# First-layer blocks in pairs: one SiLU and one block transposition over two PSUM banks

## Chip, cores and metric

The kernel runs on one core of one Trainium2 chip. Its metric is the device time of one execution in microseconds (us); the time stated for a kernel is the median of several runs. The engines are called as the profile calls them: PE (matmuls), PEld (the loading of a matmul's stationary operand, which overlaps PE), DVE (VectorE), ACT (ScalarE), POOL (GpSimd) and SP (the queue that issues the DMAs).

## The reference

A long convolution by FFT over 8 sequences of 3072 tokens with 256 channels, then a dense layer pair on all 24576 tokens, then a soft mixture of experts. Cut to what matters:

```python
X = np.fft.rfft(x, axis=1);  y = np.fft.irfft(X * (filt_r + 1j * filt_i)[None], n=3072, axis=1)
x = y.reshape(24576, 256)
h = x @ w_in                                  # 256 -> 2048
g = h * (1.0 / (1.0 + np.exp(-h)))            # SiLU
x = g @ w_out                                 # 2048 -> 256
logits = x @ phi                              # 256 -> 32 slots
d = softmax of logits over the tokens;  slot_input = d.T @ x
slot_out = per expert: relu(slot_input @ w1[e]) @ w2[e]        # 8 experts, 4 slots each
c = softmax of logits over the slots;  out = c @ slot_out
```

## The kernel before

The second dense layer is never formed for all tokens: its weights are folded with `phi` into `wp`, so that logits come straight from the SiLU outputs, and the sum over tokens is taken over the 2048 hidden values.

**Tiling.** Tokens go in 48 chunks of 512, six to a sequence. A chunk's first layer has 16 blocks m = 0 to 15 of 128 hidden values. `hidden(c, m)` makes one block: six matmuls of 128x512 into one PSUM bank of the tag "ph" (four banks). `act(c, m)` is one SiLU on ACT from that bank to a tile `g` in SBUF (tag "g", 12 buffers). `turn(c, m)` transposes `g` in blocks of 32x32 on DVE into the tile `X`. `logits(c, h)` multiplies eight `g` tiles with `wp`; `soft0` and `soft1` make the running maximum and the exponentials of the chunk (`nm`, `e`, `E`), and `dsum`, `update` the weighted sum of `X` (`pd`, `acc`). `hidden` of block m can begin only when the SiLU of block m-4 has read the bank.

**Staging.** The FFT of the next sequence runs between these blocks: `mat1` (tiles `pa`, evicted by `out1` to `ea`), `mat2` (`px`, scaled by `scale` on ACT, DVE and POOL), `mat3` (`pb`, four banks, evicted on ACT by four instructions to `eb` in `out3`). `pa`, `px` and three of the `pb` banks share three PSUM banks of the tag "pf". By the plan `mat3` stands in chunks 2 to 5, 8 to 11, and so on to 38 to 41: in 28 chunks, each time behind block 3. The exponentials of a chunk (`soft1`) are taken in the next chunk, also near block 3, and need another ACT function table than SiLU: each time a table load before and one behind. In every fourth chunk (4, 8, ... 44) a further Exp over 512 columns (`cexp`, tile `ct`) comes in there.

**What sets the order.** `at(t, fn, ...)` collects all steps with a due time in units of one block; they are written out sorted by time, and PE executes exactly that order. On ACT, DVE, POOL and SP the order is chosen by the framework's scheduler when the program is built; each of these engines then works strictly in that order. Semaphores and buffer rotation are generated.

**Tail.** After the last chunk the experts run once: `peh` (tag "ph"), ReLU to `hr`, transposition through PE (`pht`), copy to `hT`, second product (`pso`), split into `so` by quarters q. The slot softmax, parked in DRAM as `cT`, is loaded back as `cl` (tag "g") and split into `z`. The output product `po` (576 matmuls of 256 columns) alternates between "ph" and "pf" banks; DVE evicts the one half and ACT the other.

Of the kernel before, what the change touches and what calls it, by code (L numbers as in the profile page):

```python
# [27 lines left out]
CPB = NJ // JC  # L28
NB16 = TC // 32

BUFS = dict(X=2, yT=2, g=12, L=2, nm=4, E4=2, lall=2, ct=1, cm=1,
            ld=3, c=2, ch=2, xh=2, ev=2, a=2, f=2, sw=1, y=4, ev8=1, bl=1, dl=1, wt=3)


# [6 lines left out]
def fftconv_moe_softmoe(ctx, tc, x, cmat, dmat, emat, gmat, filt, filt0, w_in, w_outT,  # L41
# [6 lines left out]
    cst = ctx.enter_context(tc.tile_pool(name="cst", bufs=1))  # L48
    wk = ctx.enter_context(tc.tile_pool(name="wk", bufs=2))
    dram = ctx.enter_context(tc.tile_pool(name="dram", bufs=2, space=bass.MemoryType.DRAM))  # L50
    ps_h = ctx.enter_context(tc.tile_pool(name="ps_h", bufs=4, space=bass.MemoryType.PSUM))
    ps_1 = ctx.enter_context(tc.tile_pool(name="ps_1", bufs=1, space=bass.MemoryType.PSUM))
    ps_f = ctx.enter_context(tc.tile_pool(name="ps_f", bufs=3, space=bass.MemoryType.PSUM))
    fctx = ctx.enter_context(ExitStack())
# [94 lines left out]
    def at(t, fn, *args):  # L149
        plan.append((t, len(plan), fn, args))  # L150
# [148 lines left out]
    def fft_first():  # L299
# [4 lines left out]
        def load(v):  # L304
            tag = ("y", "y", "y", "y", "sw", "f")[v]
            cs[v] = fp.tile([P, 4, P], F32, tag=tag, bufs=BUFS[tag], name=f"c_0_{v}")
            DQ.dma_start(cs[v], cmat[:, 4 * v:4 * v + 4, :])
            for i in range(2):
                xs[2 * v + i] = wk.tile([P, 2, CH], F32, tag="g", bufs=BUFS["g"], name=f"x_0_{2 * v + i}")
                DQ.dma_start(xs[2 * v + i], xb[:, 4 * v + 2 * i:4 * v + 2 * i + 2, :])  # L310

        def loadf(i):
# [32 lines left out]
                scale(ps[r], f[:, r], y, sw, Q + U == 0)  # L345

        def second(Q):
            ps = [ps_h.tile([P, 2, CH], F32, tag="ph", name=f"pb_0_{Q}{g}") for g in range(4)]
            stage3(ps, [ys.pop((Q, U)) for U in range(4)], Q)
            if Q % 3:  # L350
                ev = wk.tile([P, 2, 4, CH], F32, tag="yT", bufs=BUFS["yT"], name=f"eb_0_{Q}")
            else:
                ev = fp.tile([P, 2, 4, CH], F32, tag="ev8", bufs=BUFS["ev8"], name=f"eb_0_{Q}")
            for g, p in enumerate(ps):
                A.activation(ev[:, :, g, :], p, AF.Copy)  # L355
            store2(s2k, ev, Q)
# [71 lines left out]

    def hidden(c, m):
        y = ytile[c]  # L430
        ph = ps_h.tile([P, TC], F32, tag="ph", name=f"ph_{c}_{m}")
        n = 0
        for h in range(2):
            for a, k in ((0, 0), (0, 1), (1, 0)):
                mm(ph, w_hl[:, a, h, m * P:(m + 1) * P], y[:, h, k, :], n == 0, n == 5)
                n += 1
        pht[c, m] = ph

    def act(c, m):
# [124 lines left out]
    for c in range(NCHUNK):  # L564
        t0 = 16 * c
        ty = t0 - 4.4 if c else -2
        if c > 0:
            at(ty - 3.8, loadd, c)
            at(ty - 3.8, load3, c)
        for h in range(2):  # L570
            at(ty + 0.8 * h, mat4, c, h)
            at(ty + 0.8 * h + 0.55, out4, c, h)
        for m in range(NM):
            t = t0 + m
            at(t, hidden, c, m)
# [249 lines left out]
```

## Time and profile before

| | before |
|---|---|
| median of 3 runs (lowest, highest) | 2046.39 us (2046.02, 2047.71) |
| the profiled execution, its own time | 2049.17 us |
| its span, first to last instruction | 2047.4 us |
| PE busy | 1926.2 us, 94% of the span |
| DVE busy | 1149.6 us, 56% |
| ACT busy | 966.8 us, 47% |
| POOL busy | 337.9 us, 17% |
| mean granted share of the TensorE clock | 0.965 |

All durations below come from the one profiled execution. Its own time is 1.8 us over its span and 2.8 us over the median. A "busy" PE is one whose modelled matmuls overlap without a gap. In rows of the timeline the first number is the start in us, the second the length in us; several instructions that follow each other are one row with a count, and a bracket names the idle time of the engine before it and who ended it. The first 130 us are the first sequence's FFT, the chunks run from there to 1935, the rest is the tail.

### The profile page before, as it was taken

What the parts mean: (1) busy time and instruction counts of PE and PEld (TensorE: products, weight loads), DVE (VectorE), ACT (ScalarE), POOL (GpSimd) and SP (SyncE); (2) the same over time, 40 slices, a digit from 0 to 9 for tenths busy, and PEclk for the clock granted to TensorE, in tenths of its full rate; (3) what the DMA queues carried; (4) which work ended last, traced back from release to release, by engine and by line L of the source; (5) the groups of instructions that cost most, each with busy time, mean ns of one, the idle gap of its engine ahead of it and who ended that gap; (6) DMA issues with size and microseconds to landing.
All of it is one profiled execution on the core that took longest, in us unless ns stands there. A gap on an engine that the chain in (4) does not pass through costs nothing. (4 is left out here: it accounts for less than half of the span.)

```text
span 2047.4 us, 53590 instructions
## 1 busy us (share of the span) xinstructions
PE 1926.2 (94%) x23264; PEld 1468.1 (72%) x23264; DVE 1149.6 (56%) x1950; ACT 966.8 (47%) x1833; POOL 337.9 (17%) x249
## 2 busy tenths in 40 slices
PE   3448999999999999999999999999999999999798
PEld 2237777777777777877777777777777777778568
DVE  1475556556566565565565566566565564554444
ACT  1344445445455454554554545545555454444234
POOL 1465111211121111211221112112121110000000
PEclk7668999999999999999999999999999999999899
DMA  9655332534244333443354334424343335110659
GB/s 291 181 178 182 87 103 81 168 119 111 80 135 139 100 104 109 157 110 88 89 160 121 101 99 131 143 82 124 86 139 95 94 95 179 39 35 24 231 206 384
DMA packets 179308, 265.08 MB, mean 129 GB/s; under 512 B 16272, under 2 KB 115712, under 8 KB 174848
## 3 DMA queue, kind: packets, MB, share of 16 engines
q1 hardware_dynamic: 179072, 261.64, 42.0%
q8 instruction: 183, 3.00, 0.6%
q14 instruction: 53, 0.43, 0.1%
HBM read 177.69 MB, written 83.89 MB: 128 GB/s over the span
## 5 line engine op out<-in xcount | busy, mean ns | idle before, releaser
L60 PE MATMUL ph<-yT,w_hl 128*128 128x512 f32 x4608 | 1153.3, 399 | 2.8 <-ACT g L441 1.9
L60 PEld LDWEIGHTS ph<-yT,w_hl 128*128 128x128 f32 x4608 | 837.6, 188 | 256.3 <-issue 77.6
L451 DVE STREAM_TRANSPOSE X<-g 128x512 f32<-128x512 f32 x768 | 530.0, 702 | 421.6 <-ACT g L441 419.6
L441 ACT ACTIVATE g<-ph 128x512 f32<-128x512 f32 x768 | 449.1, 604 | 665.8 <-PE ph L60 645.2
L182 POOL TENSOR_TENSOR sw<-sw,f 128x512 f32<-128x512 f32 x128 | 166.7, 1304 | 985.6 <-ACT sw L176 925.0
L60 PE MATMUL pd<-X,E 32*32 32x512 f32 x6144 | 221.8, 604 | 7.2 <-DMA E<-ed 7.2
L515 DVE SCALAR_TENSOR_TENSOR acc<-acc,nm,pd 128x512 f32<-128x512 f32 x188 | 127.8, 741 | 121.6 <-PE pd L60 121.6
L60 PE MATMUL pl<-g,wp 128*32 128x128 f32 x6144 | 187.6, 274 | 1.9 <-DVE acc L515 1.6
L60 PEld LDWEIGHTS pl<-g,wp 128*32 128x32 f32 x6144 | 161.8, 110 | 35.7 <-issue 19.4
L221 POOL TENSOR_TENSOR xh<-x,xh 128x512 fp32r<-128x512 f32 x84 | 123.8, 1474 | 352.5 <-DVE xh L220 348.9
L60 PEld LDWEIGHTS pd<-X,E 32*32 32x32 f32 x6144 | 119.3, 103 | 83.0 <-issue 43.4
L60 PEld LDWEIGHTS py<-d,b 128*128 128x128 f32 x768 | 101.8, 194 | 30.4 <-DMA b<-s 22.9
L60 PE MATMUL py<-d,b 128*128 128x128 f32 x768 | 102.6, 277 | 22.0 <-DMA b<-s 22.0
L181 DVE TENSOR_TENSOR y<-px,f 128x512 f32<-128x512 f32 x120 | 82.5, 691 | 60.1 <-ACT sw L176 46.2
L175 ACT ACTIVATE sw<-px 128x256 f32<-128x256 f32 x128 | 49.4, 386 | 138.1 <-DVE y L183 105.1
L183 DVE TENSOR_TENSOR y<-y,sw 128x512 f32<-128x512 f32 x128 | 93.7, 736 | 35.8 <-POOL sw L182 32.3
L60 PE MATMUL px<-a,em 48*32 48x256 f32 x2048 | 76.8, 399 | 30.1 <-DMA a<-s 20.4
L60 PE MATMUL pb<-y,gm 32*64 32x256 f32 x2048 | 73.3, 412 | 22.5 <-ACT eb L355 11.9
L60 PEld LDWEIGHTS px<-a,em 48*32 48x32 f32 x2048 | 33.1, 109 | 66.2 <-issue 35.8
L60 PE MATMUL pa<-xh,ch 128*128 128x256 f32 x504 | 76.8, 287 | 3.7 <-ACT ch L223 2.3
L60 PEld LDWEIGHTS pb<-y,gm 32*64 32x64 f32 x2048 | 47.0, 141 | 45.5 <-DVE y L183 14.9
L60 PEld LDWEIGHTS pa<-xh,ch 128*128 128x128 f32 x504 | 71.2, 191 | 11.6 <-ACT ch L223 3.6
(113 smaller groups left out, 1190.2 us busy)
## 6 DMA issues: line engine op xcount, KB each, us to landing
f<-in_filt_dram SPq DMA_DIRECT2D x112, 256.0 KB, 2.9
x<-in_x_dram SPq DMA_DIRECT2D x96, 256.0 KB, 3.5
s<-ea SPq DMA_DIRECT2D x96, 256.0 KB, 3.5
s<-eb SPq DMA_DIRECT2D x64, 384.0 KB, 5.1
b<-s SPq DMA_DIRECT2D x48, 512.0 KB, 4.2
out_dram<-ots SPq DMA_DIRECT2D x24, 1024.0 KB, 5.8
a<-s SPq DMA_DIRECT2D x112, 192.0 KB, 3.9
wt<-in_w_dram SPq DMA_DIRECT2D x14, 1024.0 KB, 12.1
```

The source lines that it names most:

```text
L60: T.matmul(o, lhsT=l, rhs=r, start=start, stop=stop)
L175: A.activation(sw[:, 0, :], p[:, 1, :], AF.Copy, scale=-1.0)
L181: V.tensor_tensor(y, p, f[:, 0, :].unsqueeze(1).to_broadcast([P, 2, CH]), op=ALU.mult)
L182: G.tensor_tensor(sw, sw, f[:, 1, :].unsqueeze(1).to_broadcast([P, 2, CH]), op=ALU.mult)
L183: V.tensor_tensor(y, y, sw, op=ALU.add)
L221: G.tensor_tensor(h[:, 1, :], tf, h[:, 0, :], op=ALU.subtract)
L441: A.activation(g, pht.pop((c, m)), AF.Silu)
L451: V.transpose(xt[c][:, m].rearrange("p b j -> p (b j)"), gt[c, m])
L515: V.scalar_tensor_tensor(out=acc[:, :, a, :], in0=acc[:, :, a, :], scalar=mrun[c][:, 3:4], in1=p, op0=ALU.mult, op1=ALU.add)
```

## The change

Two blocks share one tile of two banks. `hidden` still writes one block per call into its own bank. `act` and `turn` are called for odd m only, with the pair's first block, and take 1024 columns at once; `logits` reads halves of the pair's `g`. The tag "ph" has 2 buffers of two banks in place of 4 of one, the tag "g" 6 buffers of 1024 columns in place of 12 of 512. Other users of these tags follow: the first sequence's `x` and `pb`, the experts' `peh` (one tile for both halves n), and `po` of the output (one tile for the two products on "ph"). The tiles `hr`, `hT`, `nT`, `cl` keep 512 columns, and each takes one of the six "g" buffers.

```diff
-BUFS = dict(X=2, yT=2, g=12, L=2, ...
+BUFS = dict(X=2, yT=2, g=6, L=2, ...
-    ps_h = ctx.enter_context(tc.tile_pool(name="ps_h", bufs=4, space=bass.MemoryType.PSUM))
+    ps_h = ctx.enter_context(tc.tile_pool(name="ps_h", bufs=2, space=bass.MemoryType.PSUM))
...
     def hidden(c, m):
         y = ytile[c]
-        ph = ps_h.tile([P, TC], F32, tag="ph", name=f"ph_{c}_{m}")
+        if m % 2 == 0:
+            pht[c] = ps_h.tile([P, 2, TC], F32, tag="ph", name=f"ph_{c}_{m}")
...
-                mm(ph, w_hl[:, a, h, m * P:(m + 1) * P], y[:, h, k, :], n == 0, n == 5)
+                mm(pht[c][:, m % 2, :], w_hl[:, a, h, m * P:(m + 1) * P], y[:, h, k, :], n == 0, n == 5)
...
     def act(c, m):
-        g = wk.tile([P, TC], F32, tag="g", bufs=BUFS["g"], name=f"g_{c}_{m}")
-        A.activation(g, pht.pop((c, m)), AF.Silu)
+        g = wk.tile([P, 2, TC], F32, tag="g", bufs=BUFS["g"], name=f"g_{c}_{m}")
+        A.activation(g, pht.pop(c), AF.Silu)
...
-        V.transpose(xt[c][:, m].rearrange("p b j -> p (b j)"), gt[c, m])
+        V.transpose(xt[c][:, m:m + 2].rearrange("p m b j -> p (m b j)"), gt[c, m].rearrange("p m t -> p (m t)"))
...
             at(t, hidden, c, m)
-            at(t + 0.5, act, c, m)
-            at(t + 1.2, turn, c, m)
+            if m % 2:
+                at(t + 0.5, act, c, m - 1)
+                at(t + 1.2, turn, c, m - 1)
...
     for r in range(2):
         hT = []
+        peh = ps_h.tile([P, 2, 512], F32, tag="ph", name=f"peh_{r}")
         for n in range(2):
-            ph = ps_h.tile([P, 512], F32, tag="ph", name=f"peh_{r}{n}")
+            ph = peh[:, n]
...
+        poh = ps_h.tile([P, 2, 2, CH], F32, tag="ph", name=f"po_{i}")
         for v in range(4):
             c = 2 * i + v // 2
-            po = (ps_h, ps_f)[v % 2].tile([P, 2, CH], F32, tag=("ph", "pf")[v % 2], name=f"po_{i}_{v}")
+            po = ps_f.tile([P, 2, CH], F32, tag="pf", name=f"po_{i}_{v}") if v % 2 else poh[:, v // 2]
```

PE's order in the chunks is the same. On ACT it moves. First ACT in chunk 16, a chunk with `mat3` and the further Exp: from the last SiLU ahead of the burst to the first behind it (`g_16_2` is the tile `g` of chunk 16, block 2; now of blocks 2 and 3). Before:

```order
L441 ACTIVATE g_16_2_8250<-ph_16_2_8230 128x512
L441 ACTIVATE g_16_3_8296<-ph_16_3_8252 128x512
L480 ACT_TABLE_LOAD
L480 ACTIVATE e_15_8237,nm_15_8225<-lall_3_6894,nm_15_8225 128x128
L482 ACTIVATE nm_15_8225<-nm_14_7770,nm_15_8225 128x1
L530 ACTIVATE ct_3_8348<-ct_3_8348 128x512
L272 ACTIVATE eb_3_2_8298<-pb_3_20_8260 128x2x256
L272 ACTIVATE eb_3_2_8298<-pb_3_21_8261 128x2x256
L272 ACTIVATE eb_3_2_8298<-pb_3_22_8262 128x2x256
L272 ACTIVATE eb_3_2_8298<-pb_3_23_8263 128x2x256
L441 ACT_TABLE_LOAD
L441 ACTIVATE g_16_4_8313<-ph_16_4_8305 128x512
```

And now, on the same engine at the same place:

```order
L444 ACTIVATE g_16_2_7762<-ph_16_2_7699 128x1024
L483 ACT_TABLE_LOAD
L483 ACTIVATE e_15_7706,nm_15_7694<-lall_3_6459,nm_15_7694 128x128
L485 ACTIVATE nm_15_7694<-nm_14_7271,nm_15_7694 128x1
L533 ACTIVATE ct_3_7806<-ct_3_7806 128x512
L272 ACTIVATE eb_3_2_7764<-pb_3_20_7726 128x2x256
L272 ACTIVATE eb_3_2_7764<-pb_3_21_7727 128x2x256
L272 ACTIVATE eb_3_2_7764<-pb_3_22_7728 128x2x256
L272 ACTIVATE eb_3_2_7764<-pb_3_23_7729 128x2x256
L444 ACT_TABLE_LOAD
L444 ACTIVATE g_16_4_7785<-ph_16_4_7771 128x1024
```

The burst between the two SiLU places is the same; one SiLU of 1024 columns stands on each side of it where two of 512 stood.

Second, ACT in chunk 12, where the further Exp meets `mat1` (`pa` to `ea`, `c` to `ch`). Before:

```order
L480 ACT_TABLE_LOAD
L480 ACTIVATE e_11_6455,nm_11_6439<-lall_2_5018,nm_11_6439 128x128
L482 ACTIVATE nm_11_6439<-nm_10_5942,nm_11_6439 128x1
L441 ACT_TABLE_LOAD
L441 ACTIVATE g_12_3_6494<-ph_12_3_6477 128x512
L530 ACT_TABLE_LOAD
L530 ACTIVATE ct_2_6572<-ct_2_6572 128x512
L239 ACTIVATE ea_3_6_6513<-pa_3_6_6496 128x512
L223 ACTIVATE ch_3_8_6519<-c_3_8_6446 128x256
L441 ACT_TABLE_LOAD
L441 ACTIVATE g_12_4_6511<-ph_12_4_6503 128x512
L441 ACTIVATE g_12_5_6537<-ph_12_5_6522 128x512
```

And now:

```order
L483 ACT_TABLE_LOAD
L483 ACTIVATE e_11_6052,nm_11_6036<-lall_2_4711,nm_11_6036 128x128
L485 ACTIVATE nm_11_6036<-nm_10_5571,nm_11_6036 128x1
L533 ACTIVATE ct_2_6158<-ct_2_6158 128x512
L444 ACT_TABLE_LOAD
L444 ACTIVATE g_12_2_6088<-ph_12_2_6045 128x1024
L239 ACTIVATE ea_3_6_6105<-pa_3_6_6090 128x512
L223 ACTIVATE ch_3_8_6111<-c_3_8_6043 128x256
L444 ACTIVATE g_12_4_6127<-ph_12_4_6097 128x1024
```

The further Exp now stands with the other one, between the same two table loads: two loads fewer here. SiLU of blocks 2 and 3, half of which stood before the burst, stands behind it.

Third, PE at the start of the output product in the tail (`po_i_v` before; now `po_i` is the "ph" tile of both v = 0 and v = 2). Before:

```order
L60 MATMUL po_0_0_22449<-so_22245,z_0_22397 128x256 x2
L60 MATMUL po_0_2_22465<-so_22245,z_0_22397 128x256 x2
L60 MATMUL po_1_0_22482<-so_22245,z_0_22397 128x256 x2
L60 MATMUL po_1_2_22498<-so_22245,z_0_22397 128x256 x2
L60 MATMUL po_0_0_22449<-so_22245,z_0_22397 128x256
```

And now:

```order
L60 MATMUL po_0_20897<-so_20695,z_0_20845 128x256 x2
L60 MATMUL po_1_20929<-so_20695,z_0_20845 128x256 x2
L60 MATMUL po_0_20897<-so_20695,z_0_20845 128x256
L60 MATMUL po_1_20929<-so_20695,z_0_20845 128x256
L60 MATMUL po_0_20897<-so_20695,z_0_20845 128x256 x2
```

Two products are begun side by side where four were: the second bank of a tile is written only after the first was evicted.

## Rows read from the trace of the kernel before

**Rows 1.** The page: span, and the first layer's matmuls (busy us, mean ns).

```profile
span 2047.4 us, 53590 instructions
...
L60 PE MATMUL ph<-yT,w_hl 128*128 128x512 f32 x4608 | 1153.3, 399 | 2.8 <-ACT g L441 1.9
```

**Rows 2.** Busy time by stage, 300 to 1700 us: the sum of four stages.

```profile
sum 1400.00, PE 1396.94 PEld 1058.13 DVE 829.04 ACT 710.66 POOL 236.18; mean PE 349.23 PEld 264.53 DVE 207.26 ACT 177.66 POOL 59.05
```

**Rows 3.** Waits of PE, 300 to 1900 us: us in total, times, longest.

```profile
PE pa L60 <- ACT ch L223: 2.3, 3, 0.8
PE ph L60 <- ACT g L441: 1.9, 2, 1.6
PE pl L60 <- DVE acc L515: 1.6, 2, 1.4
```

**Rows 4.** Groups by line, 300 to 1900 us: busy us, mean ns, idle before.

```profile
L451 DVE STREAM_TRANSPOSE X<-g 128x512 f32<-128x512 f32 x700 | 483.0, 702 | 381.0 <-ACT g L441 379.1
L441 ACT ACTIVATE g<-ph 128x512 f32<-128x512 f32 x701 | 409.8, 604 | 607.7 <-PE ph L60 589.0 <-DVE X L451 16.8
...
L485 DVE STREAM_TRANSPOSE e<-e 128x128 f32<-128x128 f32 x44 | 13.7, 311 | 52.1 <-ACT e L480 51.5
L467 ACT ACTIVATE lall<-pl 128x128 f32<-128x128 f32 x44 | 12.4, 282 | 23.7 <-PE pl L60 23.7
```

**Rows 5.** Timeline of chunk 16: table loads, SiLU behind the burst, and PE.

```profile
762.56 1.28 ACT L480 ACT_TABLE_LOAD   x1 [0.38 <-DVE nm L471]
...
763.39 7.21 PE L60 MATMUL ph<-yT,w_hl 128*128 128x512 f32 x30
...
767.02 1.28 ACT L441 ACT_TABLE_LOAD   x1
...
768.32 2.06 ACT L441 ACTIVATE g<-ph 128x512 f32<-128x512 f32 x4
```

**Rows 6.** Timeline of chunk 10, ACT and PE.

```profile
542.15 0.60 ACT L441 ACTIVATE g<-ph 128x512 f32<-128x512 f32 x1
...
539.62 7.30 PE L60 MATMUL ph<-yT,w_hl 128*128 128x512 f32 x30
```

**Rows 7.** Timeline of chunk 11, the last with a third FFT stage in its sequence.

```profile
574.95 1.28 ACT L480 ACT_TABLE_LOAD   x1 [0.60 <-DVE nm L471]
...
578.23 0.60 ACT L441 ACTIVATE g<-ph 128x512 f32<-128x512 f32 x1
578.73 2.06 ACT L272 ACTIVATE eb<-pb 128x512 f32<-128x512 f32 x4
...
579.78 0.87 PE L60 MATMUL pa<-xh,ch 128*128 128x256 f32 x6
```

**Rows 8.** Timeline of chunk 12, ACT and PE.

```profile
615.59 1.28 ACT L441 ACT_TABLE_LOAD   x1
...
618.80 0.63 ACT L530 ACTIVATE ct<-ct 128x512 f32<-128x512 f32 x1
...
617.95 1.55 PE L60 MATMUL ph<-yT,w_hl 128*128 128x512 f32 x6
620.27 1.20 PE L60 MATMUL pa<-xh,ch 128*128 128x256 f32 x6 [0.76 <-ACT ch L223]
```

**Rows 9.** Timeline of chunk 44, ACT and PE.

```profile
1799.80 2.07 ACT L441 ACTIVATE g<-ph 128x512 f32<-128x512 f32 x4
...
1800.45 1.66 PE L60 MATMUL ph<-yT,w_hl 128*128 128x512 f32 x6 [1.65 <-ACT g L441]
```

**Rows 10.** Timeline of the tail: PE on the experts, ACT on the quarters, SP.

```profile
1960.83 1.93 PE L60 MATMUL pso<-wt,hT 128*32 128x256 f32 x32 [0.69 <-ACT hT L678]
...
1970.82 0.37 ACT L689 ACTIVATE so<-pso 32x256 fp32r<-32x256 f32 x1 [1.55 <-PE pso L60]
...
1972.26 0.38 ACT L689 ACTIVATE so<-pso 32x256 fp32r<-32x256 f32 x1
...
1973.84 0.38 ACT L689 ACTIVATE so<-pso 32x256 fp32r<-32x256 f32 x1
...
1940.54 29.07 SPq L698 DMA_DIRECT2D cl<-cT  x12
```

More of the change, by code (lines that the diff above doesn't have):

```diff
@@ L29 @@
 NB16 = TC // 32
-BUFS = dict(X=2, yT=2, g=12, L=2, nm=4, E4=2, lall=2, ct=1, cm=1,
+BUFS = dict(X=2, yT=2, g=6, L=2, nm=4, E4=2, lall=2, ct=1, cm=1,
             ld=3, c=2, ch=2, xh=2, ev=2, a=2, f=2, sw=1, y=4, ev8=1, bl=1, dl=1, wt=3)
@@ L307, in load @@
             DQ.dma_start(cs[v], cmat[:, 4 * v:4 * v + 4, :])
+            t = wk.tile([P, 2, 2, CH], F32, tag="g", bufs=BUFS["g"], name=f"x_0_{v}")
             for i in range(2):
-                xs[2 * v + i] = wk.tile([P, 2, CH], F32, tag="g", bufs=BUFS["g"], name=f"x_0_{2 * v + i}")
+                xs[2 * v + i] = t[:, i]
                 DQ.dma_start(xs[2 * v + i], xb[:, 4 * v + 2 * i:4 * v + 2 * i + 2, :])
@@ L347, in second @@
         def second(Q):
-            ps = [ps_h.tile([P, 2, CH], F32, tag="ph", name=f"pb_0_{Q}{g}") for g in range(4)]
+            ph = [ps_h.tile([P, 2, 2, CH], F32, tag="ph", name=f"pb_0_{Q}{g}") for g in range(2)]
+            ps = [ph[g // 2][:, g % 2] for g in range(4)]
             stage3(ps, [ys.pop((Q, U)) for U in range(4)], Q)
@@ L434, in hidden @@
             for a, k in ((0, 0), (0, 1), (1, 0)):
-                mm(ph, w_hl[:, a, h, m * P:(m + 1) * P], y[:, h, k, :], n == 0, n == 5)
+                mm(pht[c][:, m % 2, :], w_hl[:, a, h, m * P:(m + 1) * P], y[:, h, k, :], n == 0, n == 5)
                 n += 1
-        pht[c, m] = ph
     def act(c, m):
-        g = wk.tile([P, TC], F32, tag="g", bufs=BUFS["g"], name=f"g_{c}_{m}")
-        A.activation(g, pht.pop((c, m)), AF.Silu)
+        g = wk.tile([P, 2, TC], F32, tag="g", bufs=BUFS["g"], name=f"g_{c}_{m}")
+        A.activation(g, pht.pop(c), AF.Silu)
         gt[c, m] = g
@@ L456, in logits @@
         for m in range(8 * h, 8 * h + 8):
-            g = gt.pop((c, m))
+            g = gt.pop((c, m - 1)) if m % 2 else gt[c, m]
             for q in range(4):
-                mm(lg[c][S * q:S * q + S], wp[:, m, :], g[:, q * P:q * P + P], m == 0, m == NM - 1)
+                mm(lg[c][S * q:S * q + S], wp[:, m, :], g[:, m % 2, q * P:q * P + P], m == 0, m == NM - 1)
     def soft0(c):
```

## The prediction

> **What bounds the kernel now.** I read the page first: the first layer's matmuls alone take 1153.3 of 2047.4 us [rows 1]. The table of busy time by stage is next: between 300 and 1700 us PE works 1396.94 of 1400.00 us, DVE 829 and ACT 711 [rows 2]. The reader is to see 3.06 us of idle PE in 1400: PE is the bound, and what ACT or DVE save there lies beside it. Third, PE's waits: 5.8 us in all for the three longest entries, nearly the whole stock of time that could be won by removing waits [rows 3]. Last, the timelines of the places where ACT is busy with something other than SiLU, since there PE's blocks come nearest to what they wait for [rows 5 to 9].
>
> **What the change saves, and why it is not on the path.** 48 chunks times 8 pairs: 384 SiLUs and 384 transpositions fewer. ACT takes 282 ns for 128 columns and 604 for 512 [rows 4], so (604 - 282)/384 = 0.839 ns a column, and 604 + 512 x 0.839 = 1033 ns for 1024. In a row, SiLUs follow each other every (2.06 - 0.60)/3 = 0.487 us [rows 5], so a pair holds ACT 0.487 + 0.43 = 0.92 us. On DVE, 311 and 702 ns [rows 4] give 1.018 ns a column and 1223 ns for a pair, 0.52 more than one transposition now. The fixed part that a merged instruction saves is 604 - 430 = 174 ns on ACT at most and 702 - 521 = 181 ns on DVE: 384 times that is 67 and 70 us of engines that have 689 and 571 us to spare in those 1400. On PE's time it is nothing.
>
> The Trainium skill has a rule for this (Perfetto Trace Analysis, section "Optimizing Scalar/DVE Operations"): larger operations raise throughput if the engine is saturated, but "If Scalar/Vector aren't saturated, but are causing bubbles on other engines, breaking up instructions may allow work to be completed sooner." By the page's overhead of about 51 ns for a ScalarE access to PSUM, 384 x 51 ns, an estimate of 20 us, would come off if ACT set the end, and the time would be 2046 - 20 = 2026. Rows 2 show the second case, an ACT that is busy for half of the stage, and so the rule speaks against this change. The first case gets no chance of its own: an ACT or DVE that set the end would leave PE idle for more than 3 us in 1400.
>
> PE gets the same matmuls in the same order. Does it lose time at a block's boundary, which now needs a semaphore half as often? Thirty matmuls across four boundaries follow each other every (7.21 - 0.40)/29 = 0.235 us [rows 5]; six of one block every (1.55 - 0.40)/5 = 0.230 us [rows 8]. A boundary can cost (0.235 - 0.230) x 29/4 = 0.036 us at the very most; in chunk 44 six take (1.66 - 0.40)/5 = 0.252 [rows 9], so the spread between places is larger than that. I take nothing.
>
> **What it costs: two blocks must both be read before PE may go on.** Before, block m waits for SiLU of block m-4. Now the pair's first block waits for the SiLU of *both* blocks of the pair two earlier. From the SiLU's end to PE's start I take 0.05 us (1799.80 + 0.60 = 1800.40, PE starts at 1800.45 [rows 9]). In the plain run of blocks this is covered: a pair takes PE 12 x 0.235 = 2.82 us, and SiLU of the pair before needs 1.03 of it. It is uncovered where a burst (table load, Exp, table load, the four `eb`) holds ACT. There is one more delay, s: the burst's first table load waits for `nm` from DVE [rows 5, 7], which may now stand behind a transposition of 1.22 us where one of 0.70 stood. So s lies between 0 and 0.52; DVE is busy 59% of the stage, and I take 0.3.
>
> *Chunks with the third FFT stage and the further Exp (4, 8, 16, 20, 28, 32, 40: seven).* In chunk 16 PE starts block 4 at 763.39; block 8 follows 24 x 0.235 later, at 769.03. The pair (4, 5) gets its SiLU behind the second table load, at 767.02 + 1.28 = 768.30, row 768.32 [rows 5]: it ends with the hand-over at 768.32 + 1.03 + 0.05 = 769.40 + s. Wait: 0.37 + s, so 0.67, between 0.37 and 0.89. Seven times is 4.7; of the 1.9 us that PE now waits for `g` [rows 3] all but the 1.65 of chunk 44 [rows 9], 0.25, already lies there. **+4.4** (2.3 to 6.0).
>
> *Chunk 10*, where `nm` comes late: block 6 would begin at 539.62 + 12 x 0.235 = 542.44, SiLU of (2, 3) is through at 542.15 + 1.03 + 0.05 = 543.23 [rows 6]. **+0.8.**
>
> *The last third-stage chunk of a sequence (5, 11, ... 41: seven).* Here `pa` shares banks with `pb`, and waits for an `eb`. In chunk 11 SiLU stands ahead of the four `eb`: the first `eb` ends now at 578.73 + 0.60 = 579.33, and `pa` starts at 579.78 [rows 7], 0.45 later. With the pair in front the first `eb` starts 0.92 behind 578.23, at 579.15, and is through at 579.15 + 0.60 + 0.05 = 579.80 + s. Wait 0.02 + s; seven times 0.32 is **+2.2** (0.1 to 3.8).
>
> *The 13 remaining third-stage chunks.* Block 6 waits for the SiLU of (2, 3), which stands ahead of the four `eb`. With chunk 11's times it is through at 578.23 + 1.03 + 0.05 = 579.31 + s and block 6 comes where `pa` comes in chunk 11, at 579.78 [rows 7]: 0.47 us of cover, more than an s of 0.3. **+0.5** for those where `nm` is later, as in chunk 10 (0 to 1.6: up to two like chunk 10).
>
> *Chunks 12, 24, 36.* The further Exp joins the first one, two table loads fall away, and the wait of 0.76 [rows 8] with them; the three of them are the 2.3 in [rows 3]. But the Exp, 0.63, now stands before the load back: 615.59 + 0.63 + 1.28 = 617.50, SiLU of (2, 3) through at 617.50 + 1.03 + 0.05 = 618.58. Block 6 stands at 617.95 [rows 8]: it waits 0.63, a wait that was not there. Each gains 0.76 - 0.63 = 0.13; three make **-0.4**. The first load stands there behind `ch`, not behind `nm`, so I put no s on it; with s = 0.3 three make +0.5, and if block 6 is not late at all, -2.3.
>
> *Chunk 44.* PE waits 1.65 today, since the SiLU of block 4 stands behind four table loads and frees block 8 only at 1800.45 [rows 9]. All four loads stay. The pair (2, 3) takes the place of block 3's SiLU between them, 0.43 longer, and the pair (4, 5) is itself 0.43 longer than one SiLU: 1799.80 + 0.43 + 1.03 + 0.05 = 1801.31, 0.86 later. **+0.9** (0.4, if the place ahead of the loads that block 2's SiLU gives up makes them earlier, to 0.9).
>
> Sum of the chunks: 4.4 + 0.8 + 2.2 + 0.5 - 0.4 + 0.9 = **+8.4**; with s = 0, 2.3 + 0.8 + 0.1 + 0 - 0.4 + 0.9 = +3.7; with s = 0.52 and all the upper ends, 6.0 + 0.8 + 3.8 + 1.6 - 0.4 + 0.9 = +12.7.
>
> *Tail.* Three terms. The experts' products come in a changed order, with work between a transposition through PE and the product that needs its copy: of three waits of 0.69 for `hT` [rows 10] one or two may be hidden, -0.7 to -1.4. The `cl` loads on SP take single "g" buffers, of which there are now 6: of the twelve loads that start together at 1940.54 [rows 10] the later half waits until `hT` and `hr` are read; SP has nothing else behind them, but the `z` that ACT makes from them come between the quarters of `so`: 0 to +1.5, I take 0.5. The output begins with two products side by side; the quarters of `so` come 1.44 and 1.58 us apart [rows 10], and PE does half as much between two of them: 0 to +4, I take 2. Sum -1.0 + 0.5 + 2, taken as **+1** (-1.4 to +5), the lower half because nothing in the rows shows how much PE still waits between quarters.
>
> Together +9.4. On the profiled execution's own 2049.17 us that is 2058.6; that execution lies 2.8 over the median of the runs, so on the median, which is what will be compared, the forecast is 2046.4 + 9.4 = **2055.8**.
>
> **Rivals.** *No change:* `nm` is not delayed, s = 0, and the tail's terms cancel: +3.7, 2050.1. For it: DVE idles 41%, and PE's wait for ACT is short even now. Against it: chunk 16's 0.37 is there without s. *Faster:* boundaries do cost PE something that the rows can't separate from noise. At 384 boundaries with 0.036 us that is -13.8, against +3.7 from the bursts with s = 0, so 2036; at 0.02, -7.7 + 3.7, 2042. To come out faster by more than a measurement can tell, it needs (9.4 + 4.1)/384 = 0.035 us a boundary with my s, or (3.7 + 4.1)/384 = 0.02 with s = 0. Against it speak chunk 44's slower pace within one block, and an idle of 3 us in 1400, which is all that removed waits could give. *Heavier slower:* s carries on: everything that ACT and DVE hand to PE behind the burst (`sw`, `y`, `E` of the next chunk) comes half a transposition later, and finds PE waiting in each of the 31 burst chunks (28 and three): 31 x 0.52 = +16, on top of 9.4: 2072. Against it: PE waits for none of these today beyond 0.1 us, so there is cover of unknown size. That the change doesn't do what it says is excluded, as the order on the engines shows 384 instructions fewer on each.
>
> **How the numbers follow.** A measurement of this kernel can tell about 0.2%, 4.1 us. Forecast 2055.8, with 2051 (s = 0 and a tail of +1) and 2063 (s = 0.52 and a tail of +4) as its own ends: 0.60. No change, 2050 and down to 2043: 0.20. Heavier, to 2072: 0.10. Faster: 0.08. The range leaves out the faster case and the far half of the heavier one: 2045 to 2067. Faster by over 0.2%: 0.08. Within it, up to 2050.5: 0.22, the second rival with the lowest end of the forecast. Slower: 0.70.
>
> **What would show it.** In the profile of after: SiLU at 1.03 us, transposition at 1.22; ACT's and DVE's busy time down, PE's not; six table loads fewer; PE's waits for `ch` gone and those for `g` up from 1.9 to 8 or so, in the chunks named, about 0.7 each, and 2 us of new waits of `pa` for `eb`; first-layer matmuls at the same 399 ns and pace; in the output's start gaps on PE between the quarters. It is wrong if PE's waits for `g` stay at 2 (then s and the cover are misjudged), if PE's pace within blocks 0 to 15 changes, or if waits for `px`, `pl` or `pd` appear, which I priced at nothing.

## The result

The changed kernel takes 2063.08 us (median of 4 runs, 2058.29 to 2064.21) against 2046.20 of before: ratio 1.0087, 95% interval 1.0073 to 1.0100, so 15 to 20 us slower. A second set of runs gave 2061.56 against 2045.95, ratio 1.0077 (1.0056 to 1.0097). The forecast was 2055.8 (2045 to 2067); the time lies in its range and on its side, 16.9 us above the kernel before where 9.4 were forecast.

The page of the changed kernel: span, then groups with busy time, mean ns, and idle time ahead with its releaser (as [rows 1, 4]).

```profile
span 2062.4 us, 52632 instructions
...
L60 PE MATMUL ph<-yT,w_hl 128*128 128x512 f32 x4608 | 1159.1, 399 | 8.5 <-ACT g L444 7.5
...
L454 DVE STREAM_TRANSPOSE X<-g 128x1024 f32<-128x1024 f32 x384 | 476.5, 1243 | 424.4 <-ACT g L444 418.6
L444 ACT ACTIVATE g<-ph 128x1024 f32<-128x1024 f32 x384 | 394.7, 1030 | 608.4 <-PE ph L60 607.5
```

Half as many SiLUs and transpositions, of 1030 and 1243 ns; a first-layer matmul still takes 399 ns, and PE's idle time ahead of these matmuls grew from 2.8 to 8.5 us. PE's waits from 300 to 1900 us (total, times, longest; as [rows 3]):

```profile
PE ph L60 <- ACT g L444: 7.5, 12, 1.2
PE pa L60 <- ACT eb L272: 2.3, 6, 0.4
PE pl L60 <- DVE acc L518: 1.9, 1, 1.9
PE pd L60 <- issue: 1.6, 1, 1.6
```

The wait for `ch` is gone, the one for `g` is four times as long, and `pa` waits for `eb`. Where the 15.0 us between the two profiled executions (2047.4 and 2062.4 us of span) went, from the starts of the matmuls in both traces:

| stretch | before | changed | difference |
|---|---|---|---|
| start to the first block of chunk 0 | 133.1 | 128.9 | -4.2 |
| chunk 0 | 64.5 | 62.9 | -1.6 |
| chunks 1 to 46 | 1687.4 | 1699.3 | +11.9 |
| chunk 47 | 49.6 | 49.1 | -0.5 |
| `ptot` to the first output matmul | 36.7 | 36.6 | -0.1 |
| first 38 of the 576 output matmuls | 5.4 | 10.1 | +4.7 |
| the others | 64.7 | 66.4 | +1.7 |
| last output matmul to the end of the span | 6.0 | 9.4 | +3.3 |

So the chunks cost some 12 us and the output nearly 10; the first two lines gave 6 back.

**Chunks.** Chunk 16, ACT and PE (start, length; as [rows 5]):

```profile
759.53 1.28 ACT L483 ACT_TABLE_LOAD   x1 [0.32 <-DVE nm L474]
...
765.28 1.94 ACT L444 ACTIVATE g<-ph 128x1024 f32<-128x1024 f32 x2
...
759.99 5.75 PE L60 MATMUL ph<-yT,w_hl 128*128 128x512 f32 x24
766.35 1.65 PE L60 MATMUL ph<-yT,w_hl 128*128 128x512 f32 x6 [0.61 <-ACT g L444]
```

The load begins 0.46 us ahead of PE's block 4, where it was 0.83 ahead: the slip s is 0.37. SiLU of the pair (4, 5) ends at 765.28 + 1.03 = 766.31, and PE's block 8, due at 759.99 + 24 x 0.235 = 765.63, starts at 766.35. Behind the wait the six matmuls take 1.65 us, not the 1.55 of [rows 8]; what this 0.1 comes to is counted further down. Chunk 11 (as [rows 7]):

```profile
571.54 1.28 ACT L483 ACT_TABLE_LOAD   x1 [2.06 <-issue]
...
574.83 1.03 ACT L444 ACTIVATE g<-ph 128x1024 f32<-128x1024 f32 x1
575.75 2.06 ACT L272 ACTIVATE eb<-pb 128x512 f32<-128x512 f32 x4
...
572.97 3.03 PE L60 MATMUL ph<-yT,w_hl 128*128 128x512 f32 x12
576.39 0.98 PE L60 MATMUL pa<-xh,ch 128*128 128x256 f32 x6 [0.39 <-ACT eb L272]
```

Here the load is 1.43 ahead of block 4; before it was 1.97 ahead (574.95 against a block 4 at 579.78 - 2.87): s is 0.53. The first `eb` is through at 575.75 + 0.60 + 0.05 = 576.40, where `pa` was due at 572.97 + 2.87 = 575.84.

What delays the load is seen in chunk 16, 8 us earlier, on DVE and POOL:

```profile
750.97 1.25 DVE L454 STREAM_TRANSPOSE X<-g 128x1024 f32<-128x1024 f32 x1 [0.23 <-ACT g L444]
752.14 0.65 DVE L183 TENSOR_TENSOR y<-y,sw 128x512 f32<-128x512 f32 x1
...
750.10 1.29 POOL L182 TENSOR_TENSOR sw<-sw,f 128x512 f32<-128x512 f32 x1 [1.56 <-ACT sw L176]
```

POOL is through with `sw` at 750.10 + 1.29 = 751.39, but `y` stands behind the paired transposition on DVE and starts at 752.14. The next `sw` on ACT, the `lall` behind that and `nm` all come later by it.

**Output.** PE, ACT and SP at its start (as [rows 10]):

```profile
1976.64 0.74 PE L60 MATMUL po<-so,z 128*128 128x256 f32 x4 [0.52 <-ACT so L694]
1977.55 0.50 PE L60 MATMUL po<-so,z 128*128 128x256 f32 x2 [0.16 <-DVE so L695]
1978.74 1.30 PE L60 MATMUL po<-so,z 128*128 128x256 f32 x6 [0.69 <-ACT so L694]
...
1977.65 0.63 ACT L705 ACTIVATE z<-cl 128x512 fp32r<-128x512 f32 x1 [0.54 <-DMA cl<-cT]
1978.31 0.37 ACT L694 ACTIVATE so<-pso 32x256 fp32r<-32x256 f32 x1
...
1979.91 0.63 ACT L705 ACTIVATE z<-cl 128x512 fp32r<-128x512 f32 x1 [0.57 <-DMA cl<-cT]
1980.57 0.37 ACT L694 ACTIVATE so<-pso 32x256 fp32r<-32x256 f32 x1
...
1964.86 14.50 SPq L703 DMA_DIRECT2D cl<-cT  x12
```

The `cl` loads begin at 1964.86, 24 us later than in [rows 10]: the first of them now needs a "g" buffer that an expert's tile holds. On ACT two `z` wait for them, and each stands ahead of a quarter of `so` that PE waits for. And then the clock goes. Busy time by window of the changed kernel (PE, PEld, DVE, ACT, POOL, then granted clock, DMA share, GB/s):

```profile
1976.00:1986.00 10.00, 7.62 (x36) 6.67 (x36) 6.84 (x13) 3.91 (x8) 0.00 (x0) 0.69 0.55 183
```

The same of the kernel before:

```profile
1971.00:1981.00 10.00, 9.42 (x75) 9.13 (x76) 9.78 (x18) 3.84 (x9) 0.00 (x0) 1.00 0.05 19
```

Behind the short runs with gaps between them the granted clock is 0.69 over these ten us, where it was 1.00: some six tenths of them at 1.2 GHz (1 - 0.62 x 0.5 = 0.69) and the rest at 2.4. From 1981.6 to 1986.7 the output's matmuls follow each other every 0.21 us, against 0.12 before and later.

### The profile page after: what moved, and what is told of

Its sections match the earlier page's. It is cut to its first block, busy times and chain, and to the rows that moved or that the text cites. A ratio compares the mean times of both kernels' runs of the same rounds, so it can differ in the third digit from the quotient of the medians.

```text
span 2062.4 us, 52632 instructions
## 1 busy us (share of the span) xinstructions
PE 1936.8 (94%) x23264; PEld 1452.2 (70%) x23264; DVE 1108.2 (54%) x1566; ACT 901.2 (44%) x1443; POOL 329.4 (16%) x249
## 5 line engine op out<-in xcount | busy, mean ns | idle before, releaser
L454 DVE STREAM_TRANSPOSE X<-g 128x1024 f32<-128x1024 f32 x384 | 476.5, 1243 | 424.4 <-ACT g L444 418.6
L444 ACT ACTIVATE g<-ph 128x1024 f32<-128x1024 f32 x384 | 394.7, 1030 | 608.4 <-PE ph L60 607.5
L60 PEld LDWEIGHTS pd<-X,E 32*32 32x32 f32 x6144 | 105.1, 103 | 95.2 <-issue 55.0
L221 POOL TENSOR_TENSOR xh<-x,xh 128x512 fp32r<-128x512 f32 x84 | 115.6, 1376 | 351.3 <-DVE xh L220 347.2
L423 ACT ACTIVATE yT<-py 128x512 fp32r<-128x512 f32 x96 | 57.1, 595 | 77.7 <-PE py L60 77.7
L424 DVE TENSOR_TENSOR yT<-py,yT 128x512 fp32r<-128x512 f32 x96 | 64.4, 672 | 41.8 <-ACT yT L423 41.8
```

Source lines behind the costliest of these rows:

```text
L60: T.matmul(o, lhsT=l, rhs=r, start=start, stop=stop)
L221: G.tensor_tensor(h[:, 1, :], tf, h[:, 0, :], op=ALU.subtract)
L423: A.activation(y[:, half, 0, :], py, AF.Copy)
L424: V.tensor_tensor(y[:, half, 1, :], py, y[:, half, 0, :], op=ALU.subtract)
L444: A.activation(g, pht.pop(c), AF.Silu)
L454: V.transpose(xt[c][:, m:m + 2].rearrange("p m b j -> p (m b j)"), gt[c, m].rearrange("p m t -> p (m t)"))
```

## The experiments

Ratios are against the kernel before, run beside each on the same chip (medians 2045.7 to 2046.0). "Chunks" is the stretch of chunks 1 to 46, 1687.4 before and 1699.3 changed.

### The tail: t_cl, t_psum, t_both

Theory A: the `cl` loads that come late make the gaps at the start of the output. Theory B: the two-bank `po` makes them.

```diff
-            hr = wk.tile([P, 512], F32, tag="g", ...
+            hh = wk.tile([P, 2, 512], F32, tag="g", ...
+            hr = hh[:, 0]
...
-            t = wk.tile([P, 4, P], F32, tag="g", ...
+            t = hh[:, 1].rearrange("p (k q) -> p k q", q=P)
...
-        cl = wk.tile([P, TC], F32, tag="g", ...
+        if k % 2 == 0:
+            cp = wk.tile([P, 2, TC], F32, tag="g", ...
+        cl = cp[:, k % 2]
```

> Changed kernel with one edit in its tail: hr and hT share one two-block g buffer, and two cl share one, so that the cl loads get buffers as early as before. In the changed kernel the first cl load starts 24 us later than before, z waits for a cl ahead of so, and the first 38 matmuls of the output take 10.1 us against 5.5. Theory A (late cl makes the gaps at the start of the output, and the clock drop behind them): those 38 take 6 to 7 us, the last transfers still end 9 us behind the last matmul; about 4 us less than the changed kernel, 2059. Theory B (the two-bank output tile makes the gaps): the 38 stay at 10, time 2063.

```diff
     fctx.close()
+    ps_h = ctx.enter_context(tc.tile_pool(name="ps_t", bufs=4, space=bass.MemoryType.PSUM))
...
-            po = ps_f.tile(...) if v % 2 else poh[:, v // 2]
+            po = (ps_h, ps_f)[v % 2].tile([P, 2, CH], F32, tag=("ph", "pf")[v % 2], name=f"po_{i}_{v}")
```

(`peh` is on one-bank tiles again, and the two-bank pool is closed behind the chunks).

> Changed kernel with one edit in its tail: the PSUM pool is closed behind the chunks and opened again with four one-bank buffers, so that the experts' products and the output have one-bank tiles as before; cl still comes late. Theory A: the start of the output stays near 10 us for its first 38 matmuls; the 1.6 us of later gaps in the output and the 3.3 us that the last transfers end later go: 5 us less, 2058. Theory B: the start falls to about 6 as well, 9 us less, 2054.

Both together:

> Both tail edits together, the chunks in pairs as in the changed kernel. If the tail is these two things, it is that of the kernel before: 36.7 us from the last sum to the first output matmul, 70.1 to the last one, 6.0 to the end, 9.5 us less than the changed kernel, 2053.5. The chunks 1 to 46 stay 11.9 us longer than before. If something else lengthens the tail, more than 2 us of the 9.5 stay.

| kernel | `cl`, `po` | time, ratio (interval) | first 38 | others | to the end |
|---|---|---|---|---|---|
| changed | late, two banks | 2063.08, 1.0087 (1.0073 to 1.0100) | 10.1 | 66.4 | 9.4 |
| t_cl | early, two banks | 2056.44, 1.0060 (1.0041 to 1.0079) | 5.0 | 66.4 | 9.3 |
| t_psum | late, one bank | 2057.10, 1.0055 (1.0043 to 1.0067) | 7.1 | 64.7 | 6.0 |
| t_both | early, one bank | 2054.34, 1.0048 (1.0036 to 1.0060) | 4.7 | 64.7 | 5.6 |
| before | early, one bank | 2046.20 | 5.4 | 64.7 | 6.0 |

Output matmuls on PE, t_cl:

```profile
1973.58 71.40 PE L60 MATMUL po<-so,z 128*128 128x256 f32 x576 [0.52 <-ACT so L695]
```

The same, t_psum:

```profile
1977.49 1.69 PE L60 MATMUL po<-so,z 128*128 128x256 f32 x12 [0.52 <-ACT so L694]
1979.62 1.69 PE L60 MATMUL po<-so,z 128*128 128x256 f32 x12 [0.45 <-ACT so L694]
1982.51 66.83 PE L60 MATMUL po<-so,z 128*128 128x256 f32 x552 [1.20 <-ACT so L694]
```

The same, t_both:

```profile
1976.66 69.37 PE L60 MATMUL po<-so,z 128*128 128x256 f32 x576 [0.52 <-ACT so L695]
```

A holds for the start: with `cl` early PE runs through all 576 matmuls, two-bank tile or not, and with `cl` late it is held. But the tile sets how much that costs. With one-bank tiles late `cl` costs some 2.5 us (7.1 against 4.7), and the granted clock is 1.00 over the first ten us; with the two-bank tile it costs 5.1 (10.1 against 5.0), with the clock at 0.69. So half of it needs both. B holds for what follows: the two-bank tile costs 1.7 us among the later matmuls and 3.3 at the end. How the end grows is seen in the last two output transfers on SP, first of the changed kernel:

```profile
2053.15 1.62 SPq L726 DMA_DIRECT2D out_dram<-ots  x2
```

And of the kernel before:

```profile
2039.14 3.21 SPq L720 DMA_DIRECT2D out_dram<-ots  x2
```

With a two-bank `po` PE works on two transfers' worth of output at a time, and the last two are issued 0.7 us apart at the very end; before they were 2.9 apart, one of them while PE still worked. With both edits the tail is back at that of before, and 8.6 us of the time are left. In the profiles the chunks are 9.8 longer (1697.2), start and chunk 0 are 3.9 shorter.

One stretch is not in the table, `ptot` to the first output matmul: 36.6 us in the changed kernel, 33.6 in t_cl, 36.5 in t_psum, 36.2 in t_both. Most of t_cl's 3 us are not its edit. Experts on PE, changed kernel:

```profile
1953.57 4.48 PE L60 MATMUL peh<-wt,sim 128*32 128x512 f32 x18 [0.32 <-DVE sim L664]
```

The same, t_cl:

```profile
1954.16 2.34 PE L60 MATMUL peh<-wt,sim 128*32 128x512 f32 x18 [0.32 <-DVE sim L664]
```

From the first `peh` to the first `pso` the granted clock is 0.67 in the first, 1.00 in the second, and 0.81 before. In the second profile of the changed kernel (after2 below) it is 1.00 too, and the stretch takes 34.2: two executions of one kernel differ here by 2.3 us.

### What in a pair costs: c_turn2, c_silu2, c_bank1

The first two are the changed kernel, tail included. The transposition in two:

```diff
-        V.transpose(xt[c][:, m:m + 2]..., gt[c, m]...)
+        for i in range(2):
+            V.transpose(xt[c][:, m + i].rearrange("p b j -> p (b j)"), gt[c, m][:, i])
```

> Changed kernel, but the transposition of a pair in two instructions of 512 columns; SiLU stays one of 1024. Theory A (the table load of a burst slips by 0.37 to 0.53 us because nm stands behind a 1.24 us transposition on DVE): the slip goes, the seven waits of pa for eb (0.55 longer each) shrink to under 0.1, the seven of block 8 in chunks 4, 8, 16 and so on from 0.78 to 0.4, chunks 1 to 46 fall by 6 us, to some 1691 us. Theory B (the slip comes from the longer SiLU ahead on ACT): the waits stay, chunks 1 to 46 stay at 1697.

SiLU in two, the transposition in one again:

```diff
-        A.activation(g, pht.pop(c), AF.Silu)
+        ph = pht.pop(c)
+        for i in range(2):
+            A.activation(g[:, i], ph[:, i], AF.Silu)
```

> Changed kernel, but SiLU of a pair in two instructions of 512 columns on the same two-bank tile; the transposition stays one of 1024. Theory A (PE loses because both banks of a tile must be read before either is free): the second SiLU ends 0.49 + 0.60 = 1.09 us behind the start, where one of 1024 ended at 1.03, so the waits stay or grow by 0.06; chunks 1 to 46 at 1697 to 1699 us, time as the changed kernel, 2061 to 2065. Theory B (PE loses because the one SiLU is longer): block 8's waits fall by 0.4 us each, chunks 1 to 46 to 1692 or less.

The kernel before with nothing but the transposition in pairs (the paired `g` makes `cl` come late here too):

```diff
-        g = wk.tile([P, TC], F32, tag="g", ...
-        A.activation(g, pht.pop((c, m)), AF.Silu)
+        if m % 2 == 0:
+            gt[c, m] = wk.tile([P, 2, TC], F32, tag="g", ...
+        A.activation(gt[c, m - m % 2][:, m % 2], pht.pop((c, m)), AF.Silu)
...
-            at(t + 1.2, turn, c, m)
+            if m % 2:
+                at(t + 1.2, turn, c, m - 1)
```

> Kernel before with the transposition alone in pairs: one-bank products, one SiLU of 512 columns a block into half of a paired g, one transposition of 1024 on DVE; g has 6 paired buffers, so cl in the tail comes late here too. Theory A (PE loses time since it must wait until both blocks of a tile are read): PE's waits for g are back at 2 us, chunks 1 to 46 cost 0 to 3 us more than before, the tail some 4 us more by the late cl; 2050 to 2053. Theory B (the loss comes from the 1.24 us transposition that delays nm and with it the table load): the chunks still cost 6 us or more, 2056.

Measured: c_turn2 2066.43 us (1.0105, 1.0086 to 1.0124), chunks 1700.1; c_silu2 2072.79 (1.0137, 1.0118 to 1.0156), chunks 1705.4; c_bank1 2077.81 (1.0156, 1.0143 to 1.0169), chunks 1717.1. PE's waits in c_turn2, 300 to 1900 us:

```profile
PE ph L60 <- ACT g L444: 8.4, 12, 1.3
PE pa L60 <- ACT eb L272: 2.7, 6, 0.5
```

And in c_silu2:

```profile
PE ph L60 <- ACT g L446: 9.1, 13, 1.3
PE pa L60 <- ACT eb L272: 3.2, 6, 0.5
```

c_turn2 misses its theory A: the waits grew. (Neither it nor c_silu2 has a lone wait in chunk 24 that the changed kernel has, so their chunks are rather to be held against the 1697.2 of t_both.) In chunk 11 the load is 1.37 us ahead of block 4, a slip of 0.60 against 0.53. Both halves become ready when the one SiLU ends, so DVE takes them together, 0.70 and 0.60 us, and `y` stands behind them as before. It is the pair as a unit that makes the slip, not the length of one instruction. c_silu2 goes by its theory A, and further than expected: no ACT instruction is longer than before, but PE waits more. Its pair holds ACT for 1.09 where the SiLU of 1024 columns took 1.03, and the slip in chunk 11 is 0.62.

c_bank1 was expected near 2050 and took 2077.81; neither theory had named why. Chunk 16, ACT and PE:

```profile
769.88 0.60 ACT L442 ACTIVATE g<-ph 128x512 f32<-128x512 f32 x1
770.49 1.28 ACT L530 ACT_TABLE_LOAD   x1
771.79 0.63 ACT L530 ACTIVATE ct<-ct 128x512 f32<-128x512 f32 x1
...
774.38 1.28 ACT L442 ACT_TABLE_LOAD   x1
...
776.32 2.08 PE L60 MATMUL ph<-yT,w_hl 128*128 128x512 f32 x4 [3.15 <-ACT g L442]
```

The scheduler took a SiLU between the two Exps: two more table loads, and PE waits 3.15 us for `g`. It did so in the seven third-stage chunks with the further Exp (113 loads in all, 105 before): these seven are 32.5 us longer than before, all others together 2.7 shorter, and chunk 11's type, seven chunks, 0.5 longer.

### The transposition in pairs without that order: c_bank1x

`EARLY` are the chunks 3, 7, 15, 19, 27, 31 and 39.

```diff
         A.activation(L, pl, AF.Copy)
+        if c in EARLY:
+            cprep(c // 4)
         V.tensor_reduce(nm[:, 0:1], L, axis=AX.X, op=ALU.max)
...
-        if c % 4 == 0 and c // 4 - 1 in csm:
-            cexp(c // 4 - 1)
+        if c in EARLY:
+            cexp(c // 4)
+        if c % 4 == 0 and c // 4 - 1 in csm and c - 1 not in EARLY:
+            cexp(c // 4 - 1)
```

> The kernel with one-bank products and only the transposition in pairs (c_bank1) lost 3.3 us at block 8 of chunks 4, 8, 16, 20, 28, 32, 40: there the further Exp came to stand behind a SiLU and two more table loads. Here cprep stands ahead of nm in these seven chunks, so that both Exps stand between one pair of table loads (99 loads in place of 113). Theory A (that order made the whole loss): the seven waits fall to 0.5 us or less, chunks 1 to 46 from 1717 to 1688 to 1693 us, time 2048 to 2053 with the late cl in the tail. Theory B (the paired transposition itself holds ACT and PE up): the chunks stay over 1700.

Measured: 2044.89 us, ratio 1.0003 (0.9991 to 1.0015), chunks 1684.5: both below what was expected (2048 to 2053, and 1688 to 1693). PE's waits:

```profile
PE ph L61 <- ACT g L443: 1.7, 1, 1.7
PE pl L61 <- DVE acc L520: 1.5, 1, 1.5
```

384 transpositions fewer on DVE, the same 1.24 us each as in the changed kernel, and PE waits for nothing new. Counted from each matmul's start to the next one's, PE spends 1064.1 us on first-layer matmuls in chunks 1 to 46, against 1069.1 before, 1081.4 changed and 1064.6 in b_tail below, which has the short table order and no pairing: the pairing of the transposition costs the blocks nothing. The slip is there (chunk 11: 1.62 ahead of block 4, so 0.35), but with one-bank products block 6 needs block 2's SiLU alone, which was read long before the burst. So the waits of the blocks for `g` are made by the two-bank tile: its banks come free together, behind the later SiLU. The slip only sets their size. The chunks of chunk 11's type (5.0 us in seven) lose theirs in another way: `pa` waits for `eb`, and `eb` stands on ACT behind the SiLU of both blocks, as that of block 2 is now issued with that of block 3. In c_bank1x block 2's SiLU runs ahead of the burst, and the seven together lose 0.5. SiLUs issued in pairs on one-bank tiles, which would part the two causes by a run, were not tried. The scheduler merged the Exps in chunks 12, 24 and 36 here too, which gave 4.2 us; all other chunks together are 1.2 longer than before, the thirteen other third-stage chunks 0.1.

### The two-bank tile alone: p_bank2

```diff
-        ph = ps_h.tile([P, TC], F32, tag="ph", name=f"ph_{c}_{m}")
+        if m % 2 == 0:
+            pht[c] = ps_h.tile([P, 2, TC], F32, tag="ph", name=f"ph_{c}_{m}")
+        ph = pht[c][:, m % 2]
```

(The first sequence's `pb` is on two-bank tiles too; the tail has four one-bank buffers.)

> Kernel before with the two-bank tile alone: hidden writes two blocks into one tile of two banks, while SiLU and transposition stay one instruction a block of 512 columns; in the tail four one-bank buffers as before. Theory A (the loss of the chunks comes from the tile, whose banks come free only together): PE again waits for g near block 6 or 8 of the chunks with a burst, some 0.5 to 1 us each, chunks 1 to 46 take 6 to 10 us more than before, time 2052 to 2056, though no instruction is longer than before. Theory B (the loss needs the longer SiLU or transposition): chunks 1 to 46 within 3 us of before, time 2046 to 2049.

Measured: 2462.13 us, ratio 1.2026 (1.2000 to 1.2052), far off either theory. PE's waits from 300 to 2300 us:

```profile
PE ph L60 <- ACT g L444: 260.1, 193, 5.8
```

ACT and PE in one place:

```profile
905.38 0.60 ACT L444 ACTIVATE g<-ph 128x512 f32<-128x512 f32 x1 [1.85 <-PE ph L60]
906.03 3.01 PE L60 MATMUL ph<-yT,w_hl 128*128 128x512 f32 x12 [0.69 <-ACT g L444]
```

Here the SiLU of the first block reads the tile while the second block is still to be written, and the two wait for each other in turn, pair after pair (above, a SiLU ends at 905.98 and PE goes on at 906.03): the generated waits go by the tile, not by its banks. This says what the tile is, a unit of waiting, but the size belongs to this arrangement and not to the changed kernel, so it does not settle the price. That rests on c_bank1x and c_silu2, with the gap named there.

### Once more, and what to keep: after2, b_tail, x_turn

The changed kernel again:

> The changed kernel itself once more. In its first profile one wait of PE of 1.6 us inside the sum pd of chunk 24 has no releaser (chunk 24 is 2.1 us longer by it than chunks 12 and 36 would have it), and the first sequence's part is 4 us shorter than before. If these two belong to no part of the change they are gone here: chunks 1 to 46 at 1697 us, the first block at 128 to 133 us. The first 38 matmuls of the output again take 10 us with the clock down, and the last transfers end 9.3 us behind PE. Time 2061 to 2064.

Chunks 1699.4, first block at 127.6, `ptot` to the output 34.2, first 38 output matmuls 9.2, end 9.8. The lone wait in chunk 24 is there again:

```profile
1068.57 4.40 PE L60 MATMUL pd<-X,E 32*32 32x512 f32 x120
1073.90 1.06 PE L60 MATMUL pd<-X,E 32*32 32x512 f32 x8 [0.94 <-issue]
```

0.94 us where the first profile had 1.57, in the same place and with no releaser. The tail kernels (t_cl, t_psum, t_both) don't have it, and their chunks take 1697.2 to 1697.7. So it goes with this program, and the expectation that it would be gone was wrong. The prediction, too, had priced waits of `pd` at nothing.

The kernel before, unpaired, with `cprep` ahead of `nm` in chunks 11, 23 and 35 (the edit of c_bank1x) and the experts' second product one step later:

```diff
-            for k in range(4):
-                for g in range(4):
-                    mm(pso[S * g:S * g + S], t[:, k, S * g:S * g + S], ...
+            if late:
+                second(*late)
+            late = (r, n, t)
+    second(*late)
```

> Kernel before, unpaired, with two edits: cprep ahead of nm in chunks 11, 23, 35, so that the further Exp shares a pair of table loads in chunks 12, 24, 36 as in the changed kernel; and in the tail the second product of an expert group stands behind the transposition of the next one, so that PE need not wait for the copy hT. Expected: the three waits of pa for ch (0.76 each and some slow pace behind them) go, -3.5; the three waits of 0.69 for hT go, -2; time 2040. Rival: nm comes later by the 2 us of cprep and the wait only moves to block 6; then 0 for the chunks, 2044.

2039.17 us, ratio 0.9966 (0.9952 to 0.9979): faster than both kernels. The waits for `ch` and for `hT` are gone (2.3 and 2.1 us before); chunks 1681.2, `ptot` to the output 34.1 against 36.7, at nearly the same granted clock (0.80 against 0.81).

The same two edits (`cprep` ahead in ten chunks) with the transposition in pairs and `cl` early:

> What the runs leave of the change, with the two edits that helped the kernel before: only the transposition in pairs on one-bank products, cprep ahead of nm in chunks 3, 7, 11 to 39, the second product of the experts behind the next transposition, and hr with hT and two cl to one g buffer, so that cl comes early. Expected: chunks 1 to 46 at 1682 to 1685 us, the first 38 matmuls of the output at 5 us, time 2037 to 2041, as b_tail (2039): the 384 transpositions saved on DVE are worth nothing, since DVE is not on the path. If they are worth something, 2035 or less.

2044.72 us, ratio 0.9995 (0.9980 to 1.0009). The expected 2037 to 2041 was missed: chunks 1687.2, 6.0 more than b_tail, of which 3.9 lie inside `pd` and 2.2 at `pa`; and 36.3 to the output. No gain from 384 transpositions saved, at any rate.

## Why the prediction came out as it did

**Right.** The signs named came: waits for `g` of 7.5 us (8 forecast), for `eb` of 2.3 (2 forecast), 99 table loads in place of 105, and gaps at the output's start. The freed time of ACT and DVE was worth nothing: PE's matmuls keep 399 ns, and the first matmul of an odd block follows the last of the even one within 0.001 us of before (0.228 us, mean of 208 places), so the faster rival's price of a boundary is zero. The pair's sizes, 1.03 and 1.22 us forecast, are 1.030 and 1.243. The mechanism of the chunks, both blocks to be read before PE goes on, and in chunk 11's type both ahead of `eb`, is what the rows of chunks 16, 11 and 14 show, and c_bank1x and c_silu2 bear it out. By kinds of chunk:

| chunks | forecast | measured |
|---|---|---|
| third stage and further Exp (7) | +4.4 | +4.5 |
| last third-stage chunk (7) | +2.2 | +5.0 |
| the other third-stage chunks (13) | +0.5 | +3.7 |
| chunk 10 | +0.8 | 0.0 |
| 12, 24, 36 | -0.4 | -0.3 (-2.8 in t_both, which lacks the lone wait) |
| chunk 44 | +0.9 | +0.7 |
| all others | 0 | -1.7 |
| sum | +8.4 | +11.9 |

The -1.7 of the others is -2.7 inside `pd` and +1.0 in the blocks. The prediction had no term for `pd`: its matmuls take 202.2 to 204.9 us over chunks 1 to 46 in the seven profiles with the two-bank tile and SiLUs in pairs, and 205.9 to 210.7 in the others, p_bank2 left out; why was not tried.

**The total, in part luck.** The chunks cost 11.9 where 8.4 were forecast, the tail 9.6 where 1 was, and the start and chunk 0, priced at nothing, gave 5.8 back. Without that gain, for which the prediction had no term and which no run explains in full, the time would have been some 2069, outside the range of 2045 to 2067.

The rule quoted from the Trainium skill (Perfetto Trace Analysis, "Optimizing Scalar/DVE Operations") pointed the right way, as the changed kernel is 16.9 us slower. c_silu2 shows its limit: the SiLU broken up on a shared tile cost more, not less (chunks 1705.4 against 1699.3).

**The slip, mis-sized.** s was taken as 0.3 and is 0.37 in chunk 16 but 0.53 in chunk 11, the upper end. With 0.53 the step for the last third-stage chunks gives 0.02 + 0.53 = 0.55 a chunk, just the length by which `pa` comes late in chunk 11. (Chunk 41, counted there as the seventh, has no `pa`; its blocks 6 and 8 are held as in the thirteen.) For the other thirteen the working's "0.47 us of cover" is used up: in chunk 14 SiLU of (2, 3) is through at 686.87 + 1.03 + 0.05 = 687.95, with block 6 due at 685.01 + 2.82 = 687.83.

```profile
685.01 7.47 PE L60 MATMUL ph<-yT,w_hl 128*128 128x512 f32 x30
...
686.87 1.03 ACT L444 ACTIVATE g<-ph 128x1024 f32<-128x1024 f32 x1
```

Such holds are too short to be shown as idle time, but the 30 matmuls take 7.47 us where they took 7.11 in the same chunk before.

**The restart, missed.** A block that was held starts its second matmul 0.34 us behind its first, where 0.23 is usual within a run of blocks. The number was in [rows 9], six matmuls at 0.252 us, and was taken there for a spread between places. It is no price of standing still alone: before, the same 0.34 is the median behind matmuls of another product (355 blocks from 300 to 1900 us), and in the seven chunks with the further Exp block 8 had it already, in five of them without being late. New are two in each of the thirteen (26), one at `pa` in each of six of chunk 11's type (0.22 for 0.12), four in chunks 10, 41 and 44, and ten in the others: 46 in all, some 5 us.

**Chunk 10.** Its late `nm` was taken as given; in the changed kernel's order `nm` comes there as in chunk 11's type (the load is 1.43 ahead of block 4, before 0.75), and block 6 comes only 0.06 late.

**The tail, the step that failed.** +1 was forecast, +9.6 measured. The term of 2 us for two products side by side does not stand by itself: t_cl has that order, and PE does not wait. The term of 0.5 for late `cl` was the right place but ten times too small: it holds `so` back, and with the two-bank tile the clock falls too, 5.1 us between the changed kernel and t_cl, half of which needs that tile. The two-bank `po`, which makes the last transfers come in twos, was not priced at all: 1.7 + 3.3. The term of -0.7 to -1.4 for `hT` was about right but hidden: two waits of 0.69 and 0.74 are left of three of 0.69, and the lower clock on `peh` in the first profile took the gain back (36.6 us; 34.2 in the second).

**Not priced.** Start and chunk 0, 5.8 us shorter (7.1 in the second profile of the changed kernel). Start and chunk 0 together take 190.5 to 195.2 us in the seven profiles with the two-bank tile and SiLUs issued in pairs, 193.3 to 194.8 in the three with the transposition alone in pairs, 196.8 in p_bank2, 197.6 before and 196.9 in b_tail. Part of it is chunk 0's granted clock: 0.85 before (64.5 us), 0.91 changed (62.9), but 0.85 in t_psum (64.8), which has the same chunks. The rest stays open.

## What to carry to other kernels

Before merging instructions over two buffers, ask who waits for the buffers: a merged tile comes free when its last reader is through, and on a bound engine with half a us of cover that is paid at every burst. Fewer instructions on engines that are half idle buy nothing. Follow a changed tile size to every other user of its pool, down to the last transfer: nearly half of the loss was in a tail that the change only touched in passing. An order that the scheduler makes, as of two Exps around a SiLU, can outweigh the edit under test (32.5 us over seven chunks), so compare orders before comparing times.

## What the runs showed that was not expected

- A block of the first layer that was held pays some 0.11 us more between its first two matmuls (0.34 against 0.23), however short the hold: in chunk 2 block 8 came 0.02 us late and still paid it. Behind another product a block pays the same without a hold.
- Behind gaps of 0.16 to 0.96 us between runs of two to six matmuls the granted clock was 0.69 over ten us, and the matmuls followed each other every 0.21 us in place of 0.12. In t_psum, with gaps of 0.45 and 1.20 us around runs of twelve, it did not fall: its next 552 matmuls take 66.83 us, 0.121 each.
- Waits of PE with no releaser, of 0.4 to 1.6 us inside `pd` or a block, sit in one place of a program and return when it runs again (1.57 and 0.94 in chunk 24), and other builds have them elsewhere or not at all. Their cause is open.
